# Transposes by row halves, and a new order of steps on TensorE and ScalarE, in a top-k attention with a mixture of depths

## The chip, the cores and the metric

The kernel runs on one core of one Trainium2 chip. The core has a matrix engine (TensorE; PE in the profile, its weight loads PEld), a vector engine (VectorE, DVE), an engine for activations (ScalarE, ACT), a general engine (GpSimd, POOL) and SyncE (SP), which here only issues DMAs. Each engine works off its own instructions in program order, and waits on semaphores for the others. Matrix products land in PSUM, from which ScalarE and VectorE read; everything else lives in SBUF. Time is that of one execution on the device in microseconds; the median of 3 runs of the kernel before is 815.06 us (814.77 to 815.24).

## The reference

For 8 batches and 8 heads, with 576 rows and a head dimension of 64:

```python
scores = scale * np.matmul(q, k.transpose(0, 1, 3, 2))
kth = np.partition(scores, -32, axis=-1)[..., -32:-31]
scores = np.where(scores >= kth, scores, -1000000000.0)
attn = np.exp(scores - np.max(scores, axis=-1, keepdims=True))
attn = attn / (np.sum(attn, axis=-1, keepdims=True) + 1e-09)
x = np.matmul(attn, v)            # heads side by side: (8, 576, 512)
```

Every row keeps its 32 largest scores. After it comes the mixture of depths, batch by batch: a gate score per row (`x @ w_gate`), the 128 rows with the largest gate scores, and for these `x + sigmoid(score) * (relu(x @ w1) @ w2)`; w1 is 512 x 1024, w2 is 1024 x 512. The other rows go out unchanged.

## The kernel before, in words

**Units.** A batch is cut into 18 units: four tiles of 128 queries with four head pairs each, and two units for the last 64 queries. One unit is 128 rows (partitions) by two heads by 576 keys. There are 144 units, numbered through all batches.

**The pipeline.** The loop at L1108 (`for n in range(-1, N)`) writes down one step of a software pipeline by hand, and every engine keeps that order (`InOrder`, L31 to L45; since every operation is recorded there, nearly all rows of the profile have the line L45, and groups are told apart by the names of their tiles). In step n

- TensorE makes the scores of unit n+1 (`multiply`, into the PSUM tile `ps`); ScalarE copies them to SBUF (`keep`, tile `sc`).
- VectorE bounds unit n (`bound_of`, `find_bound`): maxima of seven parts of each row (MAX8, tile `cand`), and rounds on these (`best`, `bound`), which give a lower bound of the row's 32nd largest score.
- ScalarE takes signs for unit n-1 (`what_is_below`, `part`: tile `sides`, with a count read out of the accumulator), one instruction for each head. GpSimd multiplies scores and signs (tile `y`) and adds eight fill columns (`fill`).
- VectorE finds the 32nd largest in y for unit n-2 (`kth_of`, MAX8, tile `next`).
- The mask of unit n-3 (`mask_of`, tile `less`): one head on ScalarE, one on GpSimd.
- Unit n-4 is weighed (`weigh`): TensorE turns its scores so that keys lie on partitions. For each of eight 128 x 128 blocks a transpose into the PSUM tile `ptr` is followed by a matmul that adds a huge negative number where the mask is set (`turn_some`). A ninth block holds the last 64 keys of both heads (`turn_last`; it lies in the PSUM tile `av`). ScalarE takes the exponential of both (tiles `pT` and `last`), TensorE multiplies with the values (`values`, into `av`), and ScalarE copies the result (`keep_values`, tile `xs`).

The PSUM tiles `ptr`, `ps`, `av` and the bank called `misc` have one buffer each. A new tile in one of them waits for the last reader of the tile before.

**Beside it.** While one batch is computed, keys and queries of the next are loaded (SP) and turned by TensorE, half a load at a time, into free columns of `ps`, and copied by ScalarE (`qT`, `kT`). When a tile of queries is complete, GpSimd divides by the sums (`normalise`, tile `x`), and one step later VectorE makes the gate scores with one product for each tile (`gates`, `dot`: tile `prod`).

**The mixture** of a batch is a Python generator (`mixture`, L738). Each `next` issues one piece, in steps that `mix_at` lists: six pieces that count and choose rows, the places (a matmul into `av`), the fetch of the chosen rows (an indirect DMA of GpSimd), their transposes (`xe_ps`), eight pieces of the first product (`h_ps`, two pieces to a tile, then a ScalarE relu to `hT`), and eight of the second (`y_ps`, then a ScalarE scaling to `gy` and a scatter by GpSimd). Of these the last 17 fall on units 1 to 17, two batches after their own. `xe_ps`, `h_ps` and `y_ps` all lie in the bank `misc`. The copies out of that bank are put into the list `late`, and `flush()` issues them in the next step, behind the mask.

In step n the order before is, on TensorE: turn (n-4), last block, half loads, scores (n+1), values (n-4), mixture. On ScalarE: exponential, last block's exponential, mask, late copies, copies of the half loads, scores' copy, values' copy (and sums), two signs.

The last two batches' mixtures are packed closer (`mix_at_of`, L1005), up to two pieces in a step; after the loop the last four units and the last batch's mixture follow in an order of their own.

Of the kernel before, what the change touches and what calls it, by code (L numbers as in the profile page):

```python
# [31 lines left out]
J = 4  # L32
# [16 lines left out]
def kernel(  # L49
# [16 lines left out]
    NHP = H // 2  # L66
# [541 lines left out]
    def turn_some(tr, z, less):  # L608

        pe.transpose(tr, z, ident)  # L610
        if less is not None:
            pe.matmul(
                tr, less, out_of_reach, start=False, stop=True, skip_group_check=True
            )

    def room_to_turn():
        return ps_tr.tile([P, 2, J, P], FP32, name="ptr"), ps_av.tile(
            [P, 512], FP32, name="av"
        )

    def turn(z, tr, less=None):

        for i in range(2):
            for c in range(J):
                at = slice(c * P + i * R, (c + 1) * P + i * R)
                turn_some(
                    tr[:, i, c, :], z[:, i, at], None if less is None else less[:, i, at]
                )

    def turn_last(z, av, less=None):  # L630

# [106 lines left out]
    def mixture(row0, pg, rank, exact=False):  # L738
# [134 lines left out]
        for fc in range(NFC):  # L873
# [60 lines left out]
    def add_rows(gy, row_i):  # L934

        put_rows(gy, row_i, compute_op=ALU.add)
# [87 lines left out]
    for b in range(B - 1):  # L1024
        n = (b + 1) * per_batch + mix_at_of.get(b, mix_at)[6]
        mix_steps[n].remove(b)
        place_steps[n] = b
    mixtures = {}
    qkv = {0: room_for_qkv(0)}

# [15 lines left out]
    inverting = normalised = None  # L1046
    of_batch = {}
    scs, bounds, ys, next8s, masks = {}, {}, {}, {}, {}

    def is_unit(n):  # L1050
        return 0 <= n < N

    def weigh(sc, tr, av, less):

        turn(sc, tr, less)
        tr_last = turn_last(sc, av, less)
        pT = ptpool.tile([P, 2, J, P], FP32, name="pT")
        last = ptpool.tile([P, P], FP32, name="last")

        def exp():  # L1060
            act.activation(pT, tr, AF.Exp, scale=scale)
            act.activation(last, tr_last, AF.Exp, scale=scale)

        return pT, last, exp

    def bound_of(n):
        b, i = divmod(n, per_batch)
# [2 lines left out]
        find_bound(scs[n], bounds[b][:, i, :, :])  # L1070

    def what_is_below(n):
        at, sc = 2 * n, scs[n]
        b, i = divmod(n, per_batch)
        bound = bounds[b][:, i, :, :]
        sides = wkpool.tile([P, 2, S], BF16, name="sides")
        y = wkpool.tile([P, 2, S + 8], FP32, name="y")
        for i in range(2):
            part(i, sc, bound, at, sides)
            pool.tensor_tensor(y[:, i, 0:S], sc[:, i, :], sides[:, i, :], ALU.mult)  # L1080
        fill(y, at)
        ys[n] = y

    def kth_of(n):
# [23 lines left out]
    for n in range(-1, N):  # L1108
        b, i = divmod(n, per_batch)
        if i == 0 and 0 <= b < B - 1:  # L1110
            qkv[b + 1] = room_for_qkv(b + 1)
            loading = chain(
                loading, Rows(k[b + 1], q[b + 1], *qkv[b + 1][0:2]).parts()
            )
        if 0 < n + 1 < NHP:
            first_pairs.turn(n + 1)
        if n == 0:
            for hp in range(2):
                first_pairs.turn_queries(hp)
# [12 lines left out]
        if n == 1:  # L1132
            load_v(v[0], qkv[0][2])
        if n == NHP:
            load_weights()


        gating = normalised
        if inverting is not None:
            normalised = inverting[0:2]  # L1140
            vector_late.insert(0, lambda a=inverting: normalise(*a))
            inverting = None
        else:
            normalised = None
        if gating is not None:
            amid_late.append(lambda a=gating: gates(*a))

        if is_unit(n - 4):  # L1150
            tr, av = room_to_turn()
            pT, last, exp = weigh(scs.pop(n - 4), tr, av, masks.pop(n - 4))
            exp()
        if is_unit(n - 3):
            mask_of(n - 3, (act, None) if n in scatter_steps else None)
        flush()
        if is_unit(n + 1):
            b, t, g = units[n + 1]
            kT, qT = qkv[b][0:2]
            b, i = divmod(n, per_batch)  # L1160
            if n + 1 < NHP:
                ps = room_for_first_scores()
                multiply(t, g, kT, qT, ps)
                if is_unit(n - 1):
                    what_is_below(n - 1)
                stay_busy((10, 10, 20, 30)[n + 1])
            else:
                ps = room_for_scores()
                loads = list(islice(loading, first_loads[i] if b == 0 else loads_at[i]))
                halves = [ps[:, a, :, HALF : HALF + P] for a in range(2)]  # L1170
# [3 lines left out]
                for load, half in zip(loads, halves):  # L1174
                    load[1](half)
                if n == NHP - 1:
                    stay_busy(20)
            scs[n + 1] = keep(ps)
        if is_unit(n - 4):
            b4, t4, g4 = units[n - 4]  # L1180
            values(t4, g4, pT, last, av, qkv[b4][2])
            if n in place_steps:
                values_bank[0] = av
                next(mixtures[place_steps[n]])
            if g4 == 0:
# [24 lines left out]
        if is_unit(n - 1) and n + 1 >= NHP:  # L1210
            what_is_below(n - 1)

        if gating is not None:
            b, t = gating
            if t == J:
                store(out[b], of_batch[b][0])
                mixtures[b] = mixture(float(b * S), of_batch[b][1], ranks[:, b, :])
        for b in mix_steps.get(n, ()):
            next(mixtures[b], None)
        b, i = divmod(n, per_batch)  # L1220
        if i == v_at and 0 <= b < B - 1:
            load_v(v[b + 1], qkv[b + 1][2])
# [17 lines left out]

    def weigh_unit(m):
        tr, av = other_room(m) if (N - m) % 2 else room_to_turn()
        weighed[m] = *weigh(scs.pop(m), tr, av, masks.pop(m)), av

    def values_unit(m):
        pT, last, _, av = weighed[m]
# [371 lines left out]
```

## Time and profile before

| What | Value |
|---|---|
| Median of 3 runs | 815.06 us |
| The profiled execution's own time | 816.28 us |
| Its span (first to last instruction) | 814.4 us |
| VectorE busy | 783.5 us (96%) |
| TensorE busy (matmuls; weight loads) | 777.2 us (95%); 600.3 us (74%) |
| ScalarE busy | 729.5 us (90%) |
| GpSimd busy | 721.6 us (89%) |
| Granted TensorE clock | 0.998 |

Busy times are unions of instruction spans. Matmuls overlap each other, and their ends are modelled, so that TensorE's share says less than that of the other engines. In a row of the timeline the first two numbers are the start and the length in us; a bracket at its end is the idle time of that engine before, and what ended it. Rows of waits give the total in us, the number and the longest. In a table of stretches each row has the stretch, its length, the busy time of each engine with the number of its instructions, the granted clock and the share of the DMA engines.

### The profile page before, as it was taken

To read this page: it belongs to the slowest core of one execution; us is meant where nothing else is said; L and a number is where in the kernel's file an instruction comes from. 1 tells how busy PE (TensorE), PEld (TensorE's weight loads), DVE (VectorE), ACT (ScalarE), POOL (GpSimd) and SP (SyncE) were. 2 spreads that over 40 slices of the span, in tenths; PEclk is the share of its full clock that TensorE was granted. 3 is DMA by queue.
4 is the path that set the end of the run, shared out by engine and by line. 5 is a ranking of instruction groups with operands and counts; after the bars stand their busy time and mean duration, and the time that the engine had idled before them with its cause. 6 is when DMAs were issued, how large, how long until landed. Compare 5 with 4: busy or idle time off the path is not lost. (4 is left out here: it accounts for less than half of the span.)

```text
span 814.4 us, 28453 instructions
## 1 busy us (share of the span) xinstructions
PE 777.2 (95%) x10231; PEld 600.3 (74%) x10231; DVE 783.5 (96%) x4655; ACT 729.5 (90%) x1577; POOL 721.6 (89%) x722
## 2 busy tenths in 40 slices
PE   8988888888999999999999999999999999999987
PEld 6766666667887778877787777877788777867756
DVE  6999999999999999999999999999999999999962
ACT  5999999999999999999999999999999999879840
POOL 3899999999999999999999999999999999998921
PEclk9999999999999999999999999999999999999999
DMA  8931214121151123221251221512224102001021
GB/s 169 287 89 28 52 58 106 29 53 28 60 114 26 43 59 90 66 54 33 74 106 29 54 41 60 100 28 54 41 80 94 28 3 79 23 5 25 2 72 30
DMA packets 121732, 50.38 MB, mean 62 GB/s; under 512 B 116016, under 2 KB 116016, under 8 KB 120560
## 3 DMA queue, kind: packets, MB, share of 16 engines
q1 hardware_dynamic: 118368, 43.94, 22.0%
q0 software_dynamic: 1744, 4.20, 2.9%
q8 instruction: 82, 1.34, 0.7%
q14 instruction: 66, 0.54, 0.2%
q10 hardware_dynamic: 1472, 0.36, 0.2%
HBM read 36.93 MB, written 11.55 MB: 60 GB/s over the span
## 5 line engine op out<-in xcount | busy, mean ns | idle before, releaser
L45 POOL TENSOR_TENSOR y<-sc,sides 128x576 f32<-128x576 f32 x288 | 365.8, 1294 | 51.0 <-ACT sides L45 49.3
L45 DVE MAX8 cand<-sc 128x8 f32<-128x82 f32 (+1 forms) x2016 | 314.0, 227 | 4.3 <-ACT sc L45 4.2
L45 POOL TENSOR_SCALAR less<-sc,next 128x576 bf16<-128x576 f32 x135 | 233.2, 1728 | 2.2 <-DVE next L45 1.2
L45 ACT ACTIVATE sides<-sc,bound 128x576 bf16<-128x576 f32 x288 | 223.5, 791 | 0.0
L45 PE MATMUL ptr<-out_of_reach,less 128*128 128x128 bf16 x1136 | 203.3, 219 | 18.0 <-POOL less L45 17.1
L45 PE MATMUL ptr<-ident,sc 128*128 128x128 f32 x1136 | 214.6, 280 | 0.0
L45 DVE MAX8 next<-y 128x8 f32<-128x584 f32 x288 | 204.4, 751 | 0.5 <-POOL y L45 0.5
L45 PEld LDWEIGHTS av<-v,pT 128*64 128x64 f32 x4608 | 146.1, 137 | 65.9 <-ACT last L45 62.6
L45 ACT ACTIVATE pT<-ptr 128x1024 f32<-128x1024 f32 x142 | 145.3, 1024 | 39.5 <-PE ptr L45 38.5
L45 PEld LDWEIGHTS ptr<-ident,sc 128*128 128x128 f32 x1136 | 159.9, 141 | 28.2 <-issue 16.7
L45 PE MATMUL ps<-kT,qT 64*128 64x288 f32 (+1 forms) x1248 | 174.0, 425 | 0.0
L45 PE MATMUL av<-v,pT 128*64 128x65 f32 x4608 | 166.0, 224 | 8.1 <-ACT last L45 7.4
L45 PEld LDWEIGHTS <-less 128*128 128x128 bf16 x1296 | 134.4, 104 | 36.7 <-POOL less L45 24.0
L45 ACT COPY sc<-ps 128x1152 f32<-128x1152 f32 x140 | 159.1, 1137 | 0.0
L45 PEld LDWEIGHTS ps<-kT,qT 64*128 64x128 f32 (+1 forms) x1248 | 95.8, 175 | 34.5 <-issue 20.9
L45 ACT ACTIVATE less<-sc,next 128x576 bf16<-128x576 f32 x141 | 109.8, 779 | 2.9 <-DVE next L45 2.8
L45 DVE MATCH_REPLACE8 cand<-best,cand 128x21 f32<-128x21 f32 (+1 forms) x576 | 98.9, 179 | 0.0
L45 DVE MAX8 best<-cand 128x8 f32<-128x21 f32 (+1 forms) x576 | 90.3, 189 | 0.0
L45 PE MATMUL h_ps<-xeT,w 128*128 128x128 f32 x464 | 65.7, 286 | 0.0
L45 PEld LDWEIGHTS h_ps<-xeT,w 128*128 128x128 f32 x464 | 55.8, 191 | 9.1 <-issue 7.0
L45 ACT ACTIVATION_READ_ACCUMULATOR sides<-sc,bound 128x1 f32 x288 | 61.0, 212 | 0.0
L45 PE MATMUL y_ps<-w,hT 128*128 128x512 f32 x112 | 60.6, 636 | 0.0
(165 smaller groups left out, 908.3 us busy)
## 6 DMA issues: line engine op xcount, KB each, us to landing
v<-in_v_dram SPq DMA_DIRECT2D x64, 128.0 KB, 4.4
out_dram<-x SPq DMA_DIRECT2D x8, 1024.0 KB, 4.0
rows<-in_k_dram SPq DMA_DIRECT2D x56, 128.0 KB, 2.9
rows<-in_q_dram SPq DMA_DIRECT2D x56, 128.0 KB, 3.0
w<-in_moe_w_dram SPq DMA_DIRECT2D x2, 2048.0 KB
gate_row<-row_dram SPq DMA_DIRECT2D x7, 288.0 KB, 4.4
last<-in_q_dram SPq DMA_DIRECT2D x8, 128.0 KB, 3.3
vpair<-in_v_dram SPq DMA_DIRECT2D x16, 64.0 KB, 3.9
```

The lines of the kernel that those rows point to most:

```text
L45: return lambda *a, **kw: self._tc.keep_in_program_order(fn(*a, **kw))
```

## The change

Four things change in the loop.

1. `turn` handles each block as two halves of 64 rows: two transposes (rows 0 to 63 and 64 to 127) into two PSUM banks, then two matmuls with the mask. The PSUM tile is read through `by_half`, so that a half's results lie in one bank; `values` reads `pT` through the same view.
2. TensorE's order in a step becomes: turn (n-4), scores (n+1), last block (n-4), half loads, mixture, values (n-4).
3. ScalarE's first sign of unit n-1 is issued right behind the exponential (ahead of the last block's), the second behind the scores' copy.
4. Mixture pieces from the transposes of the fetched rows on (`pieces[b] > PLACES`, 7) are issued in the middle of the step, behind `flush()` and the half loads; the earlier pieces stay at its end. The scatter of `gy` is put into its list only when the scaling has been issued.

The drain of the last four units uses the new `turn`, with the last block right behind it as before.

```diff
     def turn(z, tr, less=None):
+        to = by_half(tr)                    # "p r c (b i) -> p r (c b) i"
+        halves = [slice(r * R, (r + 1) * R) for r in range(2)]
         for i in range(2):
             for c in range(J):
                 at = slice(c * P + i * R, (c + 1) * P + i * R)
-                turn_some(
-                    tr[:, i, c, :], z[:, i, at], None if less is None else less[:, i, at]
-                )
+                for r, q in enumerate(halves):
+                    pe.transpose(to[:, r, i * J + c, :], z[q, i, at], ident[q, q])
+                for r, q in enumerate(halves):
+                    if less is not None:
+                        pe.matmul(
+                            to[:, r, i * J + c, :], less[q, i, at], out_of_reach[q, q],
+                            start=False, stop=True, skip_group_check=True,
+                        )
...
-                        pT[:, i, c, r : r + R],
+                        by_half(pT)[:, r // R, i * J + c, :],
...
-        late.append(
-            lambda ps=ps: act.activation(gy, ps, AF.Copy, scale=g)
-        )
-        pool_late.append(lambda: add_rows(gy, row_i))
+        def scale_and_add():
+            act.activation(gy, ps, AF.Copy, scale=g)
+            pool_late.append(lambda: add_rows(gy, row_i))
+
+        late.append(scale_and_add)
...
             exp()
-        if is_unit(n - 3):
-            mask_of(n - 3, (act, None) if n in scatter_steps else None)
-        flush()
+        early = is_unit(n - 1) and n + 1 >= NHP
+        if early:
+            sign(n - 1, 0)
...
                 ps = room_for_scores()
-                loads = ...
-                for load, half in zip(loads, halves):
-                    load[0](half)
                 multiply(t, g, kT, qT, by_head(ps))
...
+        if is_unit(n - 4):
+            turn_rest()()                   # last block: turn and exponential
+        if is_unit(n - 3):
+            mask_of(n - 3, (act, None) if n in scatter_steps else None)
+        flush()
+        if is_unit(n + 1) and n + 1 >= NHP:
+            loads = ...                     # half loads: turn, then copy
...
+        rest = []
+        for b in mix_steps.get(n, ()):
+            if pieces.get(b, 0) > PLACES:
+                next(mixtures[b], None)
+            else:
+                rest.append(b)
+            pieces[b] = pieces.get(b, 0) + 1
+        if is_unit(n + 1):
             scs[n + 1] = keep(ps)
+        if early:
+            sign(n - 1, 1)
         if is_unit(n - 4):
             values(t4, g4, pT, last, av, qkv[b4][2])
...
-        if is_unit(n - 1) and n + 1 >= NHP:
-            what_is_below(n - 1)
+        if early:
+            weigh_signs(n - 1)              # GpSimd's products and fill
...
-        for b in mix_steps.get(n, ()):
+        for b in rest:
             next(mixtures[b], None)
```

More of the change, by code (lines that the diff above doesn't have):

```diff
@@ L619, in room_to_turn, with by_half @@
         )
+    def by_half(a):
+        return a.rearrange("p r c (b i) -> p r (c b) i", i=R)
     def turn(z, tr, less=None):
+        to = by_half(tr)
+        halves = [slice(r * R, (r + 1) * R) for r in range(2)]
         for i in range(2):
@@ L625, in turn @@
                 at = slice(c * P + i * R, (c + 1) * P + i * R)
-                turn_some(
-                    tr[:, i, c, :], z[:, i, at], None if less is None else less[:, i, at]
-                )
+                for r, q in enumerate(halves):
[3 more added lines that the diff above has]
+                        pe.matmul(
+                            to[:, r, i * J + c, :],
+                            less[q, i, at],
+                            out_of_reach[q, q],
+                            start=False,
+                            stop=True,
+                            skip_group_check=True,
+                        )
     def turn_last(z, av, less=None):
@@ L1027 @@
         place_steps[n] = b
+    PLACES, pieces = NT + 2, {}
     mixtures = {}
@@ L1048 @@
     scs, bounds, ys, next8s, masks = {}, {}, {}, {}, {}
+    sides_of = {}
     def is_unit(n):
@@ L1055, in weigh @@
         turn(sc, tr, less)
-        tr_last = turn_last(sc, av, less)
         pT = ptpool.tile([P, 2, J, P], FP32, name="pT")
@@ L1061, in exp, with turn_rest @@
             act.activation(pT, tr, AF.Exp, scale=scale)
-            act.activation(last, tr_last, AF.Exp, scale=scale)
-        return pT, last, exp
+        def turn_rest():
+            tr_last = turn_last(sc, av, less)
+            return lambda: act.activation(last, tr_last, AF.Exp, scale=scale)
+        return pT, last, exp, turn_rest
     def bound_of(n):
@@ L1072, in what_is_below, with sign, weigh_signs @@
     def what_is_below(n):
[L1073 to L1076, printed above, removed]
+        for i in range(2):
+            sign(n, i)
+        weigh_signs(n)
+    def sign(n, i):
+        b, m = divmod(n, per_batch)
+        if i == 0:
+            sides_of[n] = wkpool.tile([P, 2, S], BF16, name="sides")
+        part(i, scs[n], bounds[b][:, m, :, :], 2 * n, sides_of[n])
+    def weigh_signs(n):
+        sc, sides = scs[n], sides_of.pop(n)
         y = wkpool.tile([P, 2, S + 8], FP32, name="y")
         for i in range(2):
-            part(i, sc, bound, at, sides)
             pool.tensor_tensor(y[:, i, 0:S], sc[:, i, :], sides[:, i, :], ALU.mult)
-        fill(y, at)
+        fill(y, 2 * n)
         ys[n] = y
@@ L1151 @@
             tr, av = room_to_turn()
-            pT, last, exp = weigh(scs.pop(n - 4), tr, av, masks.pop(n - 4))
+            pT, last, exp, turn_rest = weigh(scs.pop(n - 4), tr, av, masks.pop(n - 4))
             exp()
-        if is_unit(n - 3):
-            mask_of(n - 3, (act, None) if n in scatter_steps else None)
-        flush()
+        early = is_unit(n - 1) and n + 1 >= NHP
+        if early:
+            sign(n - 1, 0)
         if is_unit(n + 1):
@@ L1159 @@
             kT, qT = qkv[b][0:2]
-            b, i = divmod(n, per_batch)
             if n + 1 < NHP:
@@ L1168 @@
                 ps = room_for_scores()
-                loads = list(islice(loading, first_loads[i] if b == 0 else loads_at[i]))
-                halves = [ps[:, a, :, HALF : HALF + P] for a in range(2)]
-                for load, half in zip(loads, halves):
-                    load[0](half)
                 multiply(t, g, kT, qT, by_head(ps))
[L1174 to L1177, printed above, removed]
+        if is_unit(n - 4):
[4 more added lines that the diff above has]
+        if is_unit(n + 1) and n + 1 >= NHP:
+            b, i = divmod(n, per_batch)
+            loads = list(islice(loading, first_loads[i] if b == 0 else loads_at[i]))
+            halves = [ps[:, a, :, HALF : HALF + P] for a in range(2)]
+            for load, half in zip(loads, halves):
+                load[0](half)
+            for load, half in zip(loads, halves):
+                load[1](half)
+            if n == NHP - 1:
+                stay_busy(20)
+        rest = []
[6 more added lines that the diff above has]
+        if is_unit(n + 1):
             scs[n + 1] = keep(ps)
+        if early:
+            sign(n - 1, 1)
         if is_unit(n - 4):
@@ L1184 @@
                 next(mixtures[place_steps[n]])
+                pieces[place_steps[n]] += 1
             if g4 == 0:
@@ L1242, in weigh_unit, with both @@
         tr, av = other_room(m) if (N - m) % 2 else room_to_turn()
-        weighed[m] = *weigh(scs.pop(m), tr, av, masks.pop(m)), av
+        pT, last, exp, turn_rest = weigh(scs.pop(m), tr, av, masks.pop(m))
+        exp_rest = turn_rest()
+        def both():
+            exp()
+            exp_rest()
+        weighed[m] = pT, last, both, av
     def values_unit(m):
```

## The prediction

> **What bounds the kernel now.** I read the page first, then the same stretches cut at whole batches, then the waits, then one unit in order of time.
>
> ```profile
> span 814.4 us, 28453 instructions
> PE 777.2 (95%) x10231; PEld 600.3 (74%) x10231; DVE 783.5 (96%) x4655; ACT 729.5 (90%) x1577; POOL 721.6 (89%) x722
> ```
>
> ```profile
> 98.56:194.19 95.63, 85.03 (x1221) 64.48 (x1221) 95.53 (x573) 90.32 (x194) 90.66 (x89) 1.00 0.23 57
> ...
> 384.69:480.57 95.88, 94.83 (x1263) 73.38 (x1265) 95.73 (x576) 91.08 (x198) 90.46 (x88) 1.00 0.27 60
> ...
> 672.36:765.80 93.44, 92.31 (x1211) 71.95 (x1211) 93.20 (x555) 82.58 (x175) 86.39 (x85) 1.00 0.12 29
> ```
>
> A row is one batch of 18 units: its length, then busy time of PE, PEld, DVE, ACT, POOL. VectorE has 0.15 us idle in a batch of 95.88, so it sets the pace and nothing that speeds up another engine shortens such a batch. But ScalarE is busy 91.08 of the same 95.88: only 4.8 us stand between it and the bound. That margin is what this change draws on.
>
> ```profile
> PEld av L45 <- ACT last L45: 62.6, 133, 1.3
> POOL y L45 <- ACT sides L45: 49.3, 62, 12.1
> ACT pT L45 <- PE ptr L45: 38.5, 83, 1.4
> ```
>
> These are the waits that the change goes for: values for the last block's exponential, GpSimd for the first sign, the exponential for the turn. VectorE is not in them: what ends them is worth nothing by itself.
>
> One unit with a mixture step (E, the start of its exponential, is 416.02):
>
> ```profile
> 416.02 1.02 ACT L45 ACTIVATE pT<-ptr 128x1024 f32<-128x1024 f32 x1 [0.50 <-PE ptr L45]
> 416.30 1.24 PE L45 MATMUL ps<-kT,qT 64*128 64x288 f32 x8
> 416.94 0.27 ACT L45 ACTIVATE last<-av 128x128 f32<-128x128 f32 x1
> 417.09 0.78 ACT L45 ACTIVATE less<-sc,next 128x576 bf16<-128x576 f32 x1
> 417.47 1.15 PE L45 MATMUL av<-v,pT 128*64 128x65 f32 x32
> 417.76 0.38 ACT L45 ACTIVATE hT<-h_ps 128x256 f32<-128x256 f32 x1
> ...
> 418.29 1.14 ACT L45 COPY sc<-ps 128x1152 f32<-128x1152 f32 x1
> ...
> 418.78 1.16 PE L45 MATMUL h_ps<-xeT,w 128*128 128x128 f32 x8
> 419.28 0.31 ACT L45 COPY xs<-av 128x130 f32<-128x130 f32 x1
> 419.44 0.82 ACT L45 ACTIVATE sides<-sc,bound 128x576 bf16<-128x576 f32 x1
> ...
> 420.80 0.28 PE L45 MATMUL ptr<-ident,sc 128*128 128x128 f32 x1
> ...
> 420.91 0.22 PE L45 MATMUL ptr<-out_of_reach,less 128*128 128x128 bf16 x1
> ...
> 421.34 1.02 ACT L45 ACTIVATE pT<-ptr 128x1024 f32<-128x1024 f32 x1 [0.23 <-PE ptr L45]
> ```
>
> Look at hT: the copy that empties the mixture's only PSUM bank ends at 418.14, E+2.12. The next mixture step writes that bank at 418.78, 0.64 us later, so it never waits.
>
> **Part 1: halves.** Eight pairs (transpose, then the matmul that pushes masked weights out of reach) now start 0.167 us apart (the next transpose starts at 420.97). After, each is two transposes of 64 columns on two row halves, then two matmuls of 64. How fast such a transpose runs is seen on the last keys' rows:
>
> ```profile
> 399.93 0.26 PEld L45 LDWEIGHTS ps<-ident,last 64*128 64x128 f32 x3 [0.16 <-issue]
> ...
> 400.11 0.14 PEld L45 LDWEIGHTS ps<-ident,last 64*128 64x128 f32 x1
> ```
>
> Four weight loads of the same form in 0.18 us: 0.06 each. Score matmuls on two row halves start 7 ns apart, so I count two halves as one. The 64-column bf16 matmul streams half of 0.055 (the 420.91 row to the next transpose), but the next transpose's 0.055 weight load hides under nothing longer, so a pair costs 0.06 + 0.055 = 0.117 at best: a gain of 8 x 0.05 = 0.40 us a unit. Bounds: 0.09 a pair (loads hidden) gives 0.62; no side-by-side, 2 x (0.06 + 0.03) = 0.18, gives a loss of 0.1. I take 0.117, the value the load row sets.
> [...]
>
> **Part 2: ScalarE's order.** Nothing is added, one sign (0.67) and its read-out (0.09) move ahead of the last block's exponential, mask, the late copies, half loads and scores' copy; sums' and values' copies go behind the second sign. So sc comes 0.76 later after E, the second sign ends some 0.2 to 0.4 earlier, and every late copy (hT, xeT, gy) ends 0.76 later: hT at E + 1.02 + 0.76 + 0.17 + 0.66 + 0.27 = E+2.88. GpSimd's first product no longer waits for the sign; it and its fill come sooner, SP's loads are issued as before. The sign's bound is a unit old and waits for nothing.
>
> **Part 3: TensorE's order.** Scores, then last block, half loads, mixture, values. The last block's exponential comes back at about E+2.0, covered by scores, loads and mixture, so the 62.6 us of waits go; TensorE's loop without waits falls from 5.32 (416.02 to 421.34) to 4.92. But the mixture step is reached sooner: scores end about 1.2 after E, last block 0.17, loads 0.23, so E+1.6, and its bank is free only at E+2.88. **TensorE waits 1.3 us with values and the next turn queued behind.** From the copy's end to the next exponential lie the same three things as from 417.47 to 421.34 (3.87), less 0.40, plus 0.05 for the semaphore and 0.1 for one uncovered weight load: 3.62. The unit takes 2.88 + 3.62 = 6.50 against ScalarE's own work in it of 5.09 (421.34 - 0.23 - 416.02): ScalarE stands 1.4. The bounds of this wait: 1.0, if TensorE's part overlaps more than in these rows, and 1.8, if no pair gets shorter.
> How often: the step waits wherever it takes a new tile in that bank, or reads xeT. Of the 17 moved steps of a batch these are the first h step (xeT) and the third, fifth and seventh, and the first y step: five. The others find the bank theirs. The nested `scale_and_add` only keeps order: gy's scaling and GpSimd's scatter (1.61 us in its queue) are issued in the unit after the step, as now; the row fetch isn't moved.
>
> **The sum**, against the profiled execution (816.28 us: span 814.44 and 1.84 around it; the median of the runs is 815.06, 1.2 less).
> - To 194.19, no matrix step of a mixture runs. What shrinks is VectorE's product with the gate weights, which waits behind GpSimd: its least is 0.677, and the eight there took 10.5, so 5.0 too much. With GpSimd earlier I take back 4; ScalarE's 90 of 95.6 lets it.
> - Batches 194.19 to 672.36 (478.2): ScalarE's busy time 89.4 + 4 x 91.07, five waits of 1.4 each (7.0) and 0.6 a batch where its units are lighter than 4.92 give 97.0 + 4 x 98.7 = 491.8. ScalarE enters ahead: the scores that VectorE takes at 194.19 were copied by 190.42, so 3.8 of it is absorbed. 488.0 - 478.2 = +9.8.
> - 672.36 to 765.80: busy 82.6; two mixtures share it, with ten waits (xeT and gy twice each, hT six times): 14.0. Four come with two steps in the unit: 3.6 more. Three more units of two steps run at 5.8 against work of 4.6: 3.5. Light units: 0.9. Sum 104.6 against 93.44: +11.2.
> - The tail: the last turns stand in ScalarE's waits of 1.00 and 0.99 for them; 0.4 off each of two or three: -1.
> Total -4 + 9.8 + 11.2 - 1 = +16: 832.3 for the profiled execution, 831 by the median.
>
> **Rivals.**
> 1. *Faster.* The waits for the bank cost no end, because ScalarE's margin holds them: if one costs under about 0.6 us (91.1 + 0.6 + 5 x 0.6 = 94.7), VectorE stays the bound in a batch. [...]
>
> ```profile
> L45 DVE CUSTOM_DVE_ANT_0 prod<-x,wg x40: 677/954/1966, 52.4 to 784.4; 128x512 f32<-128x512 f32 x32, 64x512 f32<-64x512 f32 x8
> ```
>
> The 40 (least, median, longest ns) take 42.2 us (32 of 1.059 and 8 of 1.045, by the groups) where 27.1 would do: at most 15.1 to win, and I put two thirds, 10, and the tail's 1: 804. For it speaks that VectorE is the bound now and its own work is untouched; against it, that five waits of even 1.0 eat the margin of 4.8 a batch.
> 2. *The halves don't run side by side*: a turn then costs 0.1 more than now instead of 0.40 less. Each of five units a batch is 0.5 longer, the thirteen others run at 5.4 instead of 5.06: 2.5 + 4.7 - 0.6 = 6.6 on top in each of five batches, 8.5 in the sixth, and no gains at the ends: +56, 871. Score matmuls of two row halves that start together speak against it; that no transpose on rows 64 to 127 is in the trace leaves it open.
> 3. *The wait is there, but short*: TensorE comes later to the step, or the copy is not what it waits for, and ScalarE stands 0.9 instead of 1.4. 35 waits become 0.5 cheaper: -17, so 814, about no change.
>
> **How the numbers follow.** The forecast: 0.71; its own range 820 to 846, since a pair at 0.09 takes 12 us off (25 waits by 0.22 and the light units, and 4 in the last batches) and a wait of 1.8 adds 12. Rival 1: 0.12 (800 to 808). Rival 2: 0.06. Rival 3: 0.11 (810 to 819), a third of it faster than before and a quarter within 0.2%, about what a measurement here can tell from no change (1.6 us). The range 810 to 848 leaves out rivals 1 and 2. Faster 0.12 + 0.03, same 0.03, slower the rest, 0.82.
>
> **What the profile after would show.** Right, if TensorE's weight load for h_ps waits for ScalarE's hT and xeT some five times a batch, 1.2 to 1.4 us each, if pT's wait for ptr grows from 38.5 to 70 us or more in spite of shorter turns, if the values' wait for last is nearly gone, and if VectorE stands idle for sc or y in the batches after 194 (20 us or more in all). The turn's pairs would start 0.117 apart. Wrong, if VectorE stays at 0.15 idle a batch (rival 1: prod near 0.68), if a pair takes 0.17 or more (rival 2), or if h_ps starts at once after the half loads. What I may have missed: another wait in the new ScalarE order, above all a first sign that stands for a bound that VectorE has not found yet, once VectorE itself runs late.

## The result: 3.3% slower, and where the time went

| | Before | After |
|---|---|---|
| Median, 4 runs each on one chip | 814.97 us (814.77 to 815.24) | 841.90 us (839.84 to 843.64) |
| Profiled execution; its span | 816.28 us; 814.4 us | 840.71 us; 838.9 us |
| Granted TensorE clock | 0.998 | 0.990 |
| Batches by VectorE (first bound of one to that of the next), 194.19 to 672.36 and 189.11 to 683.34 | 478.2 us | 494.2 us |

The ratio of the medians is 1.033 (95% interval 1.030 to 1.036), +26.9 us. The forecast was 831, in a range of 810 to 848. The head of the page of the kernel after:

```profile
span 838.9 us, 33288 instructions
PE 730.3 (87%) x12535; PEld 553.3 (66%) x12535; DVE 786.1 (94%) x4655; ACT 728.9 (87%) x1577; POOL 715.5 (85%) x722
```

TensorE is 47 us less busy (730.3 for 777.2) with 2304 more matmuls: the turn did become cheaper. VectorE and ScalarE have as much to do as before (786.1 for 783.5, 728.9 for 729.5), and both now stand more. Stretches of whole batches, in the columns of the prediction (length, then PE, PEld, DVE, ACT, POOL busy, clock, DMA share):

```profile
189.11:288.50 99.39, 89.62 (x1549) 67.76 (x1545) 96.01 (x574) 89.58 (x194) 89.85 (x88) 0.98 0.23 56
386.87:486.60 99.73, 89.98 (x1549) 67.92 (x1549) 96.78 (x576) 90.77 (x198) 89.62 (x88) 0.98 0.26 58
584.99:683.34 98.35, 88.62 (x1549) 66.66 (x1549) 96.05 (x577) 90.75 (x198) 89.59 (x88) 1.00 0.21 51
```

A batch took 95.88 and VectorE was idle in 0.15 of it; now it takes 98.4, or 99.4 and 99.7 where TensorE's clock falls in it (below), and VectorE is idle in 2.3 to 3.4. No engine's busy time fills a batch any more: the time is in waits between TensorE and ScalarE.

```profile
POOL y L45 <- ACT sides L45: 65.4, 54, 10.5
PEld av L45 <- ACT last L45: 62.7, 72, 1.5
...
PEld h_ps L45 <- ACT hT L45: 37.7, 21, 2.9
ACT pT L45 <- PE ptr L45: 35.4, 54, 1.0
ACT xs L45 <- PE av L45: 34.0, 40, 4.3
...
PEld h_ps L45 <- ACT xeT L45: 16.2, 7, 2.5
DVE cand L45 <- ACT sc L45: 16.0, 26, 2.1
...
PEld y_ps L45 <- ACT hT L45: 9.9, 6, 1.8
```

The h_ps rows and the y_ps row are the wait that the prediction gave: TensorE stands for ScalarE's hT and xeT before a mixture step, 34 times in all, which no row before showed. What ScalarE loses by it is in two rows, pT (the exponential waits for the turn) and xs (the copy waits for the values); what VectorE loses is in cand <- sc. One unit with such a wait, in order of time:

```profile
409.27 1.02 ACT L45 ACTIVATE pT<-ptr 128x1024 f32<-128x1024 f32 x1
...
410.19 0.77 ACT L45 ACTIVATE sides<-sc,bound 128x576 bf16<-128x576 f32 x1
...
410.25 0.22 PE L45 MATMUL av<-out_of_reach,less 128*128 128x128 bf16 x1
...
410.31 0.39 PE L45 MATMUL ps<-ident,rows 128*128 128x128 f32 x2
...
411.11 0.77 ACT L45 ACTIVATE less<-sc,next 128x576 bf16<-128x576 f32 x1
...
411.77 0.38 ACT L45 ACTIVATE hT<-h_ps 128x256 f32<-128x256 f32 x1
...
412.20 1.16 PE L45 MATMUL h_ps<-xeT,w 128*128 128x128 f32 x8 [1.51 <-ACT hT L45]
...
413.29 1.15 PE L45 MATMUL av<-v,pT 128*64 128x65 f32 x32
...
414.72 0.27 ACT L45 COPY xs<-av 128x130 f32<-128x130 f32 x1 [0.52 <-PE av L45]
...
415.77 1.02 ACT L45 ACTIVATE pT<-ptr 128x1024 f32<-128x1024 f32 x1 [0.79 <-PE ptr L45]
```

E is 409.27. The first sign stands at E+0.92, and hT, behind it and the mask, ends at E+2.88. TensorE was through with the half loads at E+1.4 and is idle for 1.51. Values start when the mixture step is through (413.29), the next turn after them, and the next exponential at E+6.50. ScalarE stands 0.52 and 0.79 in this unit, 1.31 together.

Not foreseen at all was the clock:

```profile
386.87:395.89 9.02, 8.00 (x160) 6.32 (x162) 9.02 (x62) 8.99 (x22) 7.91 (x9) 1.00 0.37 60
395.89:400.00 4.11, 1.94 (x12) 1.33 (x9) 4.08 (x25) 4.11 (x9) 4.11 (x5) 0.83 0.01 2
400.00:404.00 4.00, 4.00 (x76) 3.60 (x76) 3.96 (x23) 1.49 (x6) 4.00 (x5) 0.75 0.65 266
404.00:412.00 8.00, 6.70 (x102) 4.94 (x99) 7.67 (x53) 7.93 (x18) 5.12 (x6) 1.00 0.01 3
```

The column behind POOL's is the granted clock. In this stretch TensorE waits 2.17 us for xeT, and from 398.60 to 402.01 the granted clock is 0.50:

```profile
399.01 2.08 PE L45 MATMUL h_ps<-xeT,w 128*128 128x128 f32 x8 [2.17 <-ACT xeT L45]
```

The unit from 395.89 takes 8.04; the same unit of the next batch, with the same wait but no drop of the clock, takes 6.68 (495.63 to 502.31). It happens four times inside the kernel (from 200.6, 398.6, 685.3 and 791.1), where the profile before has one drop, at 811.8 in the tail.

Each of the four drops lasts 3.413 us in the trace, at a granted clock of 0.50, and they start at 200.62, 398.60, 685.32 and 791.13, which is 58, 84 and 31 times 3.413 apart. The first two rows are the 3.41 us right ahead of the first two drops; the last two, 28 and 29 times 3.413 behind the start at 398.60, share the wait of the next batch (496.57 to 498.74):

```profile
197.21:200.62 3.41, 1.31 (x10) 0.59 (x8) 3.38 (x18) 3.38 (x10) 3.36 (x5) 1.00 0.02 7
395.19:398.60 3.41, 1.65 (x22) 0.93 (x16) 3.38 (x20) 3.38 (x10) 3.41 (x4) 1.00 0.01 2
494.17:497.59 3.42, 2.19 (x34) 1.33 (x30) 3.39 (x22) 3.39 (x10) 3.42 (x5) 1.00 0.00 0
497.59:501.00 3.41, 2.26 (x44) 2.10 (x44) 3.41 (x27) 3.03 (x6) 3.41 (x4) 1.00 0.09 36
```

TensorE is busy for 2.19 and 2.26 us in these two, and the clock stays at 1.00; in the 3.41 us ahead of the four drops it is busy for 0.75 to 1.65. The busy time alone does not tell the cases apart: after 702.39 to 705.80, with 1.53, the clock stayed at 1.00 too.

### The profile page after: what moved, and what is told of

It is laid out like the page before. It is cut to its first block, busy times and chain, and to the rows that moved or that the text cites. A ratio compares the mean times of both kernels' runs of the same rounds, so it can differ in the third digit from the quotient of the medians.

```text
span 838.9 us, 33288 instructions
## 1 busy us (share of the span) xinstructions
PE 730.3 (87%) x12535; PEld 553.3 (66%) x12535; DVE 786.1 (94%) x4655; ACT 728.9 (87%) x1577; POOL 715.5 (85%) x722
## 3 DMA queue, kind: packets, MB, share of 16 engines
q8 instruction: 101, 1.65, 0.8%
## 5 line engine op out<-in xcount | busy, mean ns | idle before, releaser
L45 POOL TENSOR_TENSOR y<-sc,sides 128x576 f32<-128x576 f32 x288 | 371.9, 1325 | 71.4 <-ACT sides L45 65.4
L45 POOL TENSOR_SCALAR less<-sc,next 128x576 bf16<-128x576 f32 x135 | 237.4, 1759 | 8.4 <-DVE next L45 7.3
L45 ACT ACTIVATE sides<-sc,bound 128x576 bf16<-128x576 f32 x288 | 228.1, 792 | 2.0 <-DVE bound L45 1.7
L45 PEld LDWEIGHTS av<-v,pT 128*64 128x64 f32 x4608 | 148.2, 139 | 81.0 <-ACT last L45 62.7
L45 PE MATMUL av<-v,pT 128*64 128x65 f32 x4608 | 168.2, 226 | 30.4 <-ACT last L45 30.4
L45 ACT ACTIVATE pT<-ptr 128x1024 f32<-128x1024 f32 x142 | 146.2, 1030 | 36.5 <-PE ptr L45 35.4
L45 PE MATMUL ps<-kT,qT 64*128 64x288 f32 (+1 forms) x1248 | 170.3, 422 | 0.6 <-ACT sc L45 0.3
L45 PEld LDWEIGHTS <-less 64*128 64x128 bf16 (+1 forms) x2448 | 161.4, 131 | 8.6 <-POOL less L45 8.2
L45 PE MATMUL ptr<-ident,sc 64*128 64x64 f32 x2272 | 159.0, 252 | 0.0
L45 PEld LDWEIGHTS ptr<-ident,sc 64*128 64x128 f32 x2272 | 137.4, 137 | 23.8 <-issue 21.2
L45 PE MATMUL ptr<-out_of_reach,less 64*128 64x64 bf16 x2272 | 146.2, 189 | 5.9 <-POOL less L45 5.9
L45 PEld LDWEIGHTS h_ps<-xeT,w 128*128 128x128 f32 x464 | 58.6, 199 | 54.3 <-ACT hT L45 37.7
L45 ACT COPY xs<-av 128x130 f32<-128x130 f32 (+1 forms) x160 | 44.8, 280 | 34.4 <-PE av L45 34.0
L45 PE MATMUL y_ps<-w,hT 128*128 128x512 f32 x112 | 57.2, 605 | 8.5 <-ACT hT L45 8.5
```

Source lines behind the costliest of these rows:

```text
L45: return lambda *a, **kw: self._tc.keep_in_program_order(fn(*a, **kw))
```

## The experiments

My theory: the 1.3 to 1.5 us for which TensorE stands, because ScalarE's copies out of the mixture's bank are issued behind the first sign, is the price of this change; the rest of it is good or neutral. Rivals: the mixture's place ahead of the values costs by itself; the halves or the signs cost; the clock costs. Ratios are to the kernel before, run on the same chip.

### The late copies ahead of the first sign

```diff
             exp()
+        flush()
         early = is_unit(n - 1) and n + 1 >= NHP
         if early:
             sign(n - 1, 0)
...
             mask_of(n - 3, (act, None) if n in scatter_steps else None)
-        flush()
```

> The changed kernel with one line moved: flush() stands right behind the exponential, ahead of ScalarE's first sign, so the copies that empty the mixture's bank end at about E + 1.02 + 0.27 = E+1.3 (E: start of a unit's exponential) instead of E+2.9. Theory (TensorE waits for that copy, with values and the next turn behind it): TensorE reaches the step at E+1.6 and finds the bank free, its loop falls to 4.9 us, VectorE is the bound again in all batches, and its product with the gate weights waits little: 803 us (797 to 810), below the kernel before. Rival H (the halved turn, with more instructions, costs the time) and rival S (ScalarE's new order of signs starves the others): the copies are beside the point, 835 to 842.

Measured: 802.34 us (802.24 to 803.02), ratio 0.985 (0.983 to 0.986).

```profile
span 800.4 us, 33281 instructions
PE 728.9 (91%) x12535; PEld 550.5 (69%) x12535; DVE 771.5 (96%) x4655; ACT 726.2 (91%) x1577; POOL 706.5 (88%) x722
```

```profile
377.75:472.32 94.57, 89.24 (x1551) 66.98 (x1549) 94.43 (x577) 90.47 (x198) 88.22 (x88) 1.00 0.26 61
```

One line moved, and 39.6 us come back. TensorE waits 6.4 us for hT in all instead of 37.7, and VectorE is again idle for 0.14 of a batch. That batch is 1.3 shorter than before's, and so is VectorE's busy time in it; over the kernel it fell by 12.0 (783.5 to 771.5); the medians differ by 12.6. Where it fell is VectorE's product with the gate weights (least, median, longest ns). Of this kernel:

```profile
L45 DVE CUSTOM_DVE_ANT_0 prod<-x,wg x40: 669/682/1590, 51.0 to 770.2; 128x512 f32<-128x512 f32 x32, 64x512 f32<-64x512 f32 x8
```

The median product took 954 ns before, and the 40 took 42.2 us in all; here they take 30.4. The length goes with the instruction of GpSimd that runs at the time. Of the kernel before:

```profile
399.62 2.52 POOL L45 TENSOR_TENSOR y<-sc,sides 128x576 f32<-128x576 f32 x2
...
401.27 1.42 DVE L45 CUSTOM_DVE_ANT_0 prod<-x,wg 128x512 f32<-128x512 f32 x1
```

GpSimd's products into y end at 402.14, and VectorE's product, begun in their midst, ends 0.55 later. Before, 34 of the 40 start so, and all 34 end 0.55 to 0.56 after such a product has ended. Here one of the 40 does; 37 run beside GpSimd's half of the mask (`less`) and take 0.67 to 1.01 (in the kernel after 18 do, with 0.67 to 1.03). So the order that was meant for GpSimd and TensorE pays, in the end, through an instruction of VectorE that is longer beside GpSimd's products into y: rival 1's price (804), and from the 40 products that rival 1 named, once the wait for the bank is gone. This kernel is faster than both.

### The same copies half way

```diff
             turn_rest()()
+        flush()
         if is_unit(n - 3):
             mask_of(...)
-        flush()
```

`turn_rest()()` issues the last block's exponential, so hT now ends at E+2.2, between the 1.28 of the run above and the 2.88 of the change.

> The changed kernel with flush() between the last block's exponential and the mask: the copy that empties the mixture's bank ends at E + 1.02 + 0.76 + 0.17 + 0.27 = E+2.2, between the E+1.3 of copies_first (802.3) and the E+2.9 of the changed kernel (841.9). Theory (the wait's length decides, once ScalarE's margin is used up): a unit with a wait takes 2.2 + 3.6 = 5.8 instead of 6.5, a batch some 95.1 against VectorE's own 94, and the clock does not fall in waits of hT: 810 us (805 to 818), nearer to copies_first than the middle of the two. A rival by which each microsecond of wait costs the same all the way: 802.3 + 39.6 x (2.2 - 1.3) / (2.9 - 1.3) = 825.

Measured: 815.99 us (10 runs, 814.26 to 816.71), ratio 1.0005 (0.9995 to 1.0015): no change. Units that wait for hT take 5.80 to 5.84, those between them 4.85 to 4.97. By the prediction's own sum a copy that ends at E+2.22 gives 2.22 + 3.62 = 5.84. The price is not linear: 0.94 later than E+1.28 costs 13.7 us, the next 0.66 cost 25.9. That fits the margin of the first paragraph of the prediction: ScalarE has some 4 us to spare in a batch, and five stands of 0.7 use them up. Batches without a fall of the clock show it by themselves: 94.6 in the run above, 95.2 here, 98.4 in the change, so that the first 0.94 costs 0.6 a batch and the next 0.66 costs 3.2, about five times itself. Falls of the clock are in the 13.7 too, which I had not expected here: the granted clock is 0.992 where copies_first has 0.998, and two units of the batches take 7.52 and 7.59 where the same unit otherwise takes 6.02, some 3 us.

### The mixture back at the step's end

```diff
-            if pieces.get(b, 0) > PLACES:
+            if False:
```

> The changed kernel with all mixture pieces back at the end of the step, behind the values. Theory: the waits for hT and xeT go, but TensorE now reaches the values at E+1.6 and the last block's exponential, behind the first sign, is back at E+2.0 only; from there 3.47 us to the next exponential, so 5.49 in 17 of 18 units, 98.2 a batch against 95.9 before: 828 us (820 to 835), with the values' wait for last at 60 us or more and none for hT. Rivals H and S: 838 to 845.

Measured: 836.76 us (835.85 to 837.85), ratio 1.027 (1.025 to 1.029). I had expected 828: this was a miss. There is no wait for hT now, but others take its place:

```profile
PEld av L45 <- ACT last L45: 109.8, 140, 2.0
...
ACT pT L45 <- PE ptr L45: 63.9, 97, 2.1
```

Values come straight behind the half loads, at about E+1.5, and the last block's exponential, behind the first sign, ends at E+1.95. TensorE waits in all 140 units that go through the loop in this order, and nearly every unit with a mixture step takes 5.53 to 5.57, where the change has 6.46 to 6.50 and 4.85 to 4.97 in turn for eight units of a batch. A batch is 99.58. So the rival that blames the mixture's new place is not borne out in this order of TensorE and ScalarE: with the mixture back the kernel is only 5 us faster, less than the 8.0 that filling the waits gives in the next run, and the stand has only another owner.

### The clock held up

```diff
             if pieces.get(b, 0) > PLACES:
+                if pieces[b] == PLACES + 2 or (pieces[b] == PLACES + 1 and b > B - 4):
+                    for _ in range(40):
+                        pe.matmul(ps[:, 0, 0, HALF + P : 512], out_of_reach, ...)
                 next(mixtures[b], None)
```

Forty small matmuls (1.86 us) into columns that nobody reads fill part of TensorE's longest waits: those for xeT, and in the last batches' mixtures also those ahead of the transposes.

> The changed kernel with 40 small matmuls on TensorE, 1.7 us in all, in the longest waits (for xeT, and in the last batches for gy). They write free columns of the scores' tile that nothing reads. In the changed kernel the granted clock falls to half for 3.4 us four times, after waits of over 2 us, and such a unit takes 8.0 us instead of 6.7. Theory (the clock falls because TensorE stands idle): the drops inside the loop go, each worth some 1.4 us: 837 us (835 to 839), clock 0.995 or more, and runs that differ by under 2 us. Rival (the long units have another cause, the clock only goes with them): 840 to 844.

Measured: 833.90 us (833.77 to 838.42), ratio 1.025 (1.022 to 1.028), 3 us below what I expected. Of the kernel with the filling, the step that the drop had hit:

```profile
394.02 1.86 PE L45 MATMUL ps<-out_of_reach 128*128 128x96 bf16 x40
396.36 1.16 PE L45 MATMUL h_ps<-xeT,w 128*128 128x128 f32 x8 [0.47 <-ACT xeT L45]
```

The eight matmuls of the step take 1.16, as everywhere, where the drop had made them 2.08. The unit takes 6.68 (exponentials at 393.24 and 399.92). The only drop left is at 831.3, behind the last matmuls. So TensorE got more work and the kernel became 8.0 us faster. Not all of that is the clock. If each of the four drops costs the 1.36 of this one (8.04 less 6.68), they are 5.4. In the three batches without a drop the filled kernel is 0.5 shorter too (97.85 for 98.37): one exponential in each (287.01 in the first) no longer starts 0.75 late. What it waited for I can't say; its turn had ended. So some 5 of the 26.9 are the clock, by this estimate, and the rest is the waits and what else the filling shifts.

### The signs back behind the values' copy

```diff
-        if early:
-            sign(n - 1, 0)
...
-        if early:
-            sign(n - 1, 1)
...
-            weigh_signs(n - 1)
+            what_is_below(n - 1)
```

> The changed kernel with both signs back behind the values' copy. Theory: the bank is free 0.76 us sooner (E+2.5), but ScalarE then stands some 0.4 us in each unit for the last block, which now comes behind the scores: 5.5 us a unit and five waits that are shorter by half: 845 us (836 to 856). Rival S: with the signs back the loss is gone, 812 to 820. Rival H: 838 to 845, as the changed kernel.

Measured: 869.08 us (863.83 to 870.34), ratio 1.065 (1.061 to 1.069): 24 us above what I expected.

```profile
POOL y L45 <- ACT sides L45: 104.0, 82, 10.4
ACT xs L45 <- PE av L45: 69.4, 55, 6.2
PEld L45 <- POOL less L45: 57.0, 83, 2.1
...
DVE next L45 <- POOL y L45: 43.3, 44, 7.2
```

```profile
431.95 1.22 PE L45 MATMUL ps<-kT,qT 64*128 64x288 f32 x8
432.48 1.01 ACT L45 ACTIVATE pT<-ptr 128x1024 f32<-128x1024 f32 x1
...
434.37 0.37 ACT L45 ACTIVATE hT<-h_ps 128x256 f32<-128x256 f32 x1
...
434.79 1.16 PE L45 MATMUL h_ps<-xeT,w 128*128 128x128 f32 x8 [1.08 <-ACT hT L45]
```

hT ends at E+2.3 here, for want of a sign ahead of it, but the exponential itself starts late, behind the signs of the unit before (the scores of TensorE start at 431.95, E is 432.48), so that TensorE still waits 1.08 for hT (434.79). The values, behind the mixture step, are late, and the values' copy stands in front of both signs. When it waits, the signs wait, then GpSimd's products, and VectorE stands 43 us for y. I had counted the wait and not what is queued behind it. So the new place of the signs is worth 27 us in this TensorE order.

### The mixture alone, on the kernel before

```diff
+        for b in mix_steps.get(n, ()):
+            if pieces.get(b, 0) > PLACES:
+                next(mixtures[b], None)
...
+        if is_unit(n + 1):
             scs[n + 1] = keep(ps)
...
-        for b in mix_steps.get(n, ()):
+        for b in rest:
             next(mixtures[b], None)
```

> The kernel before with one thing added: the last 17 mixture pieces are issued ahead of the values instead of behind them. Theory: TensorE reaches the step at E+1.45, the bank is free at E+2.12, and the next exponential comes at E+6.2 instead of E+5.33 in the units with a wait: 0.86 for each of 25 (21 us) and 10 in the last batches, with no spare in the loop of before: 843 us (832 to 850). Rivals H and S: the order of mixture and values alone costs nothing, 812 to 820.

Measured: 875.54 us (872.73 to 877.29), ratio 1.075 (1.073 to 1.077): 32 us above what I expected. The same chain as in the run above:

```profile
POOL y L45 <- ACT sides L45: 112.4, 98, 10.3
ACT xs L45 <- PE av L45: 93.4, 101, 3.5
DVE next L45 <- POOL y L45: 46.4, 51, 4.4
```

### The mixture and the signs, on the kernel before

To test that chain, the last kernel again with both signs between the scores' and the values' copies:

```diff
         if is_unit(n + 1):
             scs[n + 1] = keep(ps)
+        if is_unit(n - 1) and n + 1 >= NHP:
+            for i in range(2):
+                sign(n - 1, i)
```

> mixture_only (875.5 us where 843 were expected) with both signs issued ahead of the values' copy instead of behind it. In mixture_only ScalarE waits 93 us for values that now come behind the mixture, the signs are queued behind that copy, and VectorE waits 46 us for y. Theory (the surplus of some 30 us is this second wait): with the signs ahead only the five waits for the bank are left, 845 us (834 to 855), and VectorE's wait for y is gone. Rival (the waits for the bank cost more than I worked out): 868 to 878.

Measured: 860.65 us (860.14 to 862.37), ratio 1.056 (1.054 to 1.058), where I had expected 845. VectorE's wait for y is down from 46.4 to 2.6, and 14.9 us with it, about half of what mixture_only was above its forecast. Much of the other half is seen in the units without a wait for the bank (a batch is 102.4 where 95.9 and five times 0.86, 100.2, was counted). The exponential of one:

```profile
429.50 1.02 ACT L45 ACTIVATE pT<-ptr 128x1024 f32<-128x1024 f32 x1 [0.66 <-PE ptr L45]
```

The one before was at 424.02: 5.48, where I had counted 5.32 as in the kernel before. The waiting unit is as worked out, 6.19 (417.83 to 424.02).

### Without the halves

Two kernels with the turn of before in whole blocks: the change, and the kernel with the late copies first. And the halves alone on the kernel before. For the first two the diff against their own kernel is

```diff
-                for r, q in enumerate(halves):
-                    pe.transpose(to[:, r, i * J + c, :], z[q, i, at], ident[q, q])
-                ...
+                turn_some(tr[:, i, c, :], z[:, i, at], None if less is None else less[:, i, at])
...
-                        by_half(pT)[:, r // R, i * J + c, :],
+                        pT[:, i, c, r : r + R],
```

and halves_only is the kernel before with these lines the other way round.

> The changed kernel with the turn of before: whole blocks, one transpose and one matmul each, and the layout of before. Theory: the halves save 0.40 us of TensorE in each unit and the rest of the change needs it: 25 waiting units 0.4 longer (10), the others bound by a TensorE loop of 5.3 (some 20), 7 in the last batches: 878 us (868 to 888). Rival H: the loss shrinks or goes, 815 to 835.

> copies_first (802.3 us) with the turn of before, whole blocks. Theory: no wait for a copy, but TensorE's loop is back at 5.3 us in the 17 units with a mixture step, some 95.3 a batch against VectorE's own 94: 811 us (805 to 818), so that the halves are worth 9 of the 12.6 us that copies_first gains. Rival (the gain comes from the new order alone, the halves are hidden behind VectorE): 801 to 804.

> The kernel before with the halved turn alone (and the layout that goes with it). Theory: TensorE's loop falls from 5.32 to 4.9 us, no step waits for a copy (hT ends at E+2.1, the step is reached at E+2.7), VectorE keeps the bound and loses most of the 15 us that its product with the gate weights waits for GpSimd: 803 us (797 to 810). Rival H: more instructions, 815 or slower.

Measured:

| Kernel | Median, us | Ratio (95%) | Units with a step of the first product | The halves are worth |
|---|---|---|---|---|
| whole_turn | 886.27 | 1.088 (1.085 to 1.090) | 5.39 to 5.44; waiting for hT 6.91 to 6.95 | 44.4, against after |
| copies_first_whole | 828.17 | 1.015 (1.014 to 1.017) | 5.39 to 5.44 | 25.8, against copies_first |
| halves_only | 808.27 | 0.991 (0.990 to 0.993) | VectorE sets the pace (0.14 idle in a batch of 94.47) | 6.4, against before |

I had expected 878, 811 and 803. One edit, three prices. On the kernel before VectorE has 0.15 idle in a batch and the halves can only give GpSimd and `prod` some air (VectorE busy 783.5 to 777.2); in the new order TensorE's loop is on the path and each of the 0.4 to 0.5 us of a unit counts. Of the kernel with the copies first but whole blocks:

```profile
384.19:482.54 98.35, 97.35 (x1264) 72.58 (x1262) 96.42 (x576) 90.96 (x198) 91.03 (x88) 1.00 0.25 59
```

TensorE is busy for 97.35 of 98.35. The 811 came of a loop of 5.32 as before; it is 5.42. Both kernels with whole blocks in the new order, and mixture_signs, have 5.39 to 5.48. What they share is the number of times that TensorE goes from one shape of weights to another in a unit (the figures behind the operation's name in the rows: 128\*128, 64\*128 for scores and halves, 128\*64 for values). The kernel before goes from 128\*128 to 64\*128 to 128\*64 and back, three changes; these have four, because scores and values no longer lie next to one another. The kernel after, where the halves have the shape of the scores that follow, has three, and 4.85 to 4.97, as forecast from 5.32. The fourth change then goes with 5.39 to 5.48 less 5.32, 0.07 to 0.16 us a unit. That it is the change of shape that costs this is an estimate of mine from these unit lengths; it was not measured by itself. What the traces show of it is idle time of the weight loads: in the kernel before they stand 0.17 us ahead of a unit's scores for nothing that the profile shows (22.8 us in all, 138 times), in the kernel after, where the shape there stays the same, 17 times (3.0 us).

## Why the prediction was right, point by point

**The bound and the wait.** The mechanism came out as written: copies at E+2.88 (2.88), waiting units of 6.50 (6.46 to 6.50; those that wait for xeT 6.68), the units between them 4.92 (4.85 to 4.97), pairs of turn steps 0.117 apart (0.117 to 0.12: turn starts at 402.90, 403.02, 403.14, 403.26), ScalarE idle 1.4 in a waiting unit (1.31). TensorE's own wait was longer than the 1.3 given, since it is through with the half loads at E+1.4 and not E+1.6: 1.51 for hT in the unit shown, 2.17 for xeT. From hT's end to the mixture's first matmul lie the 0.05 counted for the semaphore (412.15 to 412.20), from there to the next exponential 3.57 (3.62 was given for both). The copies_first run shows that the wait is the cause: without it, 39.6 us less. copies_middle shows that its size follows the place of the copy.

**The sum, term by term**, in profiled executions:

| Term | Forecast, us | Measured, us |
|---|---|---|
| To the 36th unit | -4 | -5.1 (189.11 against 194.19) |
| The five batches | +9.8 | +16.1 (494.2 against 478.2) |
| The rest, with the tail | +10.2 | +13.5 (155.5 against 142.1) |
| Sum | +16 | +24.4 |

The first term holds. The eight products with the gate weights up to there took 7.1 us for 10.5, so that 3.3 came of them where 4 was given. Some 1.1 of the 5.1 is not the change's: the bound of the first unit begins at 8.16 for 9.22, but also in mixture_only, which up to its 36th unit runs in the order of before, it begins at 7.85.

Two terms were mis-sized.

*The lead.* ScalarE's own sum for the five batches was 491.8; the batches took 494.2, and without the two drops of the clock in them (some 2.7) 491.5. But I let 3.8 of it be "absorbed", since ScalarE enters ahead of VectorE. It enters ahead, and stays ahead: the scores that VectorE takes first have been ready for 3.75 us in the first of these batches, for 3.17 to 3.20 at the begin of each later one, and for 3.19 behind the last, so 0.6 was spent and not 3.8. In the batch from 386.87 the lead falls from 3.19 to 0.03 in the first units and grows from 0.06 to 3.02 over the last five, which are light: it is paid out and earned back in each batch. A lead absorbs a loss only if it is smaller at the end.

*The clock.* No drop was foreseen. Four drops of 1.36, the estimate of above, are 5.4: 2.7 in the batches, 2.7 in the rest. With these and the whole lead the forecast would have been 16 + 3.8 + 5.4 = 25.2, against 24.4.

**Rivals.** Rival 1 has the right price for the wrong kernel: with no long wait, 802.3 (804 forecast). Its point of decision, 0.6 a wait, lies where copies_middle stands: 0.7 a wait gave the time of before. Rival 2, halves one after the other, is out by the pairs 0.117 apart, and by the 44 us that the halves save here; its price was also summed wrongly, for 16 + 5 x 6.6 + 8.5 and 5 for the lost gains at the ends is 62 and not 56. Rival 3, ScalarE standing only 0.9, is out by the 1.31 measured.

**Where a sign in the profile was foretold wrongly.** pT's wait for ptr was to be 70 us or more; it is 35.4, and xs's wait for av, 2.0 before, is 34.0. Their sum is 69.4: I had the whole stand in one place, but the values' copy is the first instruction of ScalarE that meets it. The values' wait for last was to vanish; it is as large as before (62.7, in 72 units instead of 133). I had it covered by scores, loads and mixture. Of the 72 units 38 have no mixture step ahead of their values, and hold 38.1 of it; in the other 34 a step of the second product stands there, and the next weight load is idle, mostly for 0.76, while TensorE's matmuls still run. It can have cost little: copies_first has 84.7 of it and is the fastest. VectorE's idle time came for sc, as foretold, but 20 us or more for sc and y were given, and it is 16.0 and 1.7, and 6.4 for the sums. And TensorE's waits for hT and xeT were to be 1.2 to 1.4 each; they are 1.4 to 1.5 and 2.1 to 2.3 in the batches.

## What to carry to other kernels

When an instruction is moved ahead of others on an in-order engine, list what was behind it that empties a buffer with one copy, and set the time at which each such copy now ends against the time at which the other engine wants the buffer; here one line, the copies first, makes 841.9 into 802.3. Price a wait with everything that is queued behind the waiting instruction: the change cost 27 us more with both signs behind the copy that waits for the values. And an engine's slack can be spent once per batch only if it isn't already spent in that batch; a lead at the start is no slack if it is there again at the end.

## What the runs showed of the hardware

- The granted TensorE clock of the kernel after fell to 0.50 for 3.413 us four times, each time in or right behind a wait of TensorE of 2.17 to 2.66 us (until 200.83, 399.01, 685.07 and 790.60), while waits of 2.17 (until 498.74) and 1.91 (until 704.27) passed at 1.00. The starts of the drops lie 58, 84 and 31 times 3.413 us apart, and in the 3.41 us before one TensorE had been busy for 0.75 to 1.65. Why one wait brought a drop and another of its length did not is not shown. In the unit concerned a drop cost 1.36 us (8.04 less 6.68); forty matmuls without a use (1.86 us), put in the gap, took the drops away, and the kernel became 8.0 us faster.
- Two transposes of 64 rows and the two matmuls with the mask on them take 0.12 us a pair (402.90 to 403.26 in the kernel after, three pairs) where one of 128 rows and its matmul took 0.17 (420.80 to 420.97 in the kernel before), on the same data.
- A product on VectorE (`prod`, 32 of 128x512 and 8 of 64x512) took 0.68 us at its least in the kernel before and 0.67 in the kernel after. Beside GpSimd's `less` it took 0.68 to 1.16 in the kernel before (4 times) and 0.67 to 1.03 in the kernel after (18 times); when it started during GpSimd's products into y, 34 times in the kernel before, it ended 0.55 to 0.56 after one of these had ended, and took up to 1.97. Its median was 954 ns before and 682 in copies_first, with GpSimd's products issued earlier. The 40 of them took 11.8 us less, nearly the whole gain of the fastest kernel, although no wait of VectorE shows it: it is counted as busy.
